# A linear-attention and adapter kernel on one core: the r*k product written over the growth factors of the tile in front, and a new order of the steps

## The chip, the cores and the metric

The kernel runs on one core of a Trainium2 chip. Its metric is the device time of one launch in microseconds (us), the median of several runs. A core has a matrix engine (TensorE, PE in the profile), a vector engine (VectorE, DVE), an activation engine (ScalarE, ACT), a general engine (GpSimd, POOL) and a queue engine (SyncE, SP), each with its own instruction queue that is worked off in order. SBUF is the on-chip memory, PSUM the memory that TensorE writes.

## The reference

The first half is a linear attention with a state that decays per channel (batch 4, 8 heads, 768 steps, head size 48). Its output, plus a mixture of low-rank adapters over 3072 rows of 384, is the result:

```python
for t in range(S):
    kt, vt, rt, wt = k[:, :, t], v[:, :, t], r[:, :, t], w[:, :, t]
    cur = np.einsum('bhd,bhe->bhde', u[None] * kt, vt)
    y[:, :, t] = np.einsum('bhd,bhde->bhe', rt, state + cur)
    state = wt[:, :, :, None] * state + np.einsum('bhd,bhe->bhde', kt, vt)
...
logits = x @ w_gate                      # x: y as rows of 384; 8 experts
topk = np.argpartition(-logits, 2, axis=1)[:, :2]
w = softmax(logits[topk])
delta = sum over the two experts of w[k] * ((x @ A[e]) @ B[e])
return x + delta
```

(The last lines are shortened to what they compute.)

## The kernel before

The 4 x 768 steps are cut into 24 tiles of 128 steps, six for each batch element; a tile holds all 8 heads, 384 columns. Each tile goes through a row of small steps, functions named in the text ORDER: an item `mult.6` is the step `mult` of tile 6. The program is issued in exactly that order, so each engine's queue is the sequence of the items that go to it. The table ENGINES says, by one letter for each tile, which engine does a step that could go to several: D is VectorE, A ScalarE, P GpSimd. The letters of `xkev` start at tile -3.

The steps of tile t, with the line numbers of the profile:

- Loads. `load_w` (SyncE queue), `load_rk` and `load_v` (GpSimd queue, several tiles at a time, converting to 16 bits). Tiles 0 and 1 of r and k come in 32 bits (`load_rkf`, `rk_first`).
- `ln` (ScalarE) takes the logarithm of w for two tiles; `cs` and `ci` (TensorE) sum it up in PSUM; `grow` (L308) and `exps` (L319) on ScalarE turn the two sums into the two halves of a tile `e2` of growth factors, one for r and one for k, in 16 bits.
- `mult` (L336, VectorE) is the decay product: r and k by the two halves of `e2`, in one instruction; `multr` and `mult` of tile 0 do it in two halves (L322). `tr` (L389) transposes the result on TensorE, `trev` copies it out of PSUM (`rkT`; L272 on ScalarE, L274 on VectorE), `amm` (L407) multiplies r with k for each head, and `aev` (L413, VectorE) masks that to `at`.
- `rkp` (L344) is the product r*k of the tile, without growth factors, on VectorE or GpSimd. `xk` of tile t-3 (L466, TensorE) transposes it together with `xs` of tile t-3, `xkev` copies both out, `dgmm` (L349) multiplies with u, `dgev` (two tiles at a time) copies the result `dg` out, and `dv` (L361, GpSimd) multiplies v by it. That is the term of u k v.
- `kv` (L424) adds k v to the state in PSUM, `sev` copies it out; `ymm` (L445, L451) makes the output of the tile, and `xev` (L457, VectorE) adds `dv` to it, which gives `xs`.
- The adapters: `lgmm` the logits, then for four tiles at once (three and one at the end) `gate` (ScalarE, Exp), `gmax` and `gsel` (VectorE, the two best experts), `gmul` (GpSimd, the weights), `zmm` (TensorE), `zw` (VectorE), `zT` and `zTev` (transposed), then for each tile `dmm` (TensorE), `oev` (the result, L592 on VectorE or L590 on ScalarE) and `store` (SyncE queue).

The tile `rkp` has three buffers of its own and `e2` two. A step that writes a buffer waits, by a semaphore, for the readers of what was there.

Of the kernel before, what the change touches and what calls it, by code (L numbers as in the profile page):

```python
# [58 lines left out]
grow.15 xk.11 oev.5 rkp.16 trev.13 dgev.13 xkev.11 dv.12 dmm.7 ci.15 exps.15 dv.13 aev.12 rkp.17 store.2 amm.13
kv.13 oev.6 tr.14 cs.16 sev.13 lgmm.11 oev.7 load_w.20 ymm.12 trev.14 kv.14 aev.13 load_w.22 amm.14 grow.16 zmm.11  # L60
store.3 ci.16 gate.11 xev.12 ln.20 store.4 sev.14 gmax.11 mult.15 exps.16 gsel.11 aev.14 xk.12 tr.15 gmul.11 ymm.13
cs.17 zw.11 mult.16 xkev.12 dgmm.14 trev.15 grow.17 rkp.18 dgmm.15 kv.15 dgev.15 amm.15 ci.17 sev.15 zT.11 tr.16
# [6 lines left out]
xk.17 aev.19 xkev.17 dv.18 tr.20 ymm.18 trev.20 xev.18 rkp.22 zT.15 ci.22 dv.19 lgmm.17 dgmm.20 amm.20 rkp.23
zTev.15 mult.21 store.5 dmm.12 exps.22 aev.20 sev.20 dmm.13 xk.18 oev.12 xkev.18 tr.21 oev.13 ymm.19 trev.21 xev.19  # L70
lgmm.18 cs.23 grow.23 dgmm.21 store.6 amm.21 xk.19 ci.23 ymm.20 dgev.21 dmm.14 xkev.19 mult.22 dv.20 exps.23 aev.21
oev.14 dmm.15 xev.20 dv.21 lgmm.19 gate.19 mult.23 tr.22 trev.22 ymm.21 xk.20 amm.22 kv.21 oev.15 gmax.19 xev.21
xkev.20 sev.21 gsel.19 tr.23 zmm.19 gmul.19 aev.22 trev.23 zw.19 dgmm.22 dgmm.23 dgev.23 amm.23 kv.22 xk.21 zT.19
# [64 lines left out]
def kernel(  # L138
# [167 lines left out]
    def grow(t):  # L306
        e2 = wk.tile([L, 2, HD], BF16, name="e2", bufs=E2_BUFS)
        nc.scalar.activation(out=e2[:, 0], in_=cs_ps[:, 0:HD], func=ACT.Exp)  # L308
        st[t]["e2"] = e2
# [30 lines left out]
        st[t]["rk2"] = rk2  # L340

    def rkp(t):
        p_ = wk.tile([L, HD], FP16, name="rkp", bufs=3)
        (nc.gpsimd if ENGINES["rkp"][t] == "P" else nc.vector).tensor_mul(p_, st[t]["rk"][:, 0], st[t]["rk"][:, 1])  # L344
# [313 lines left out]
```

## Time and profile before

| | |
|---|---|
| median of 3 runs | 94.6 us (93.82 to 94.7) |
| the profiled execution | 93.72 us, with a span of 92.0 us from its first to its last instruction |
| mean granted TensorE clock | 0.991 |
| loads and stores | 17.53 MB in packets, mean 191 GB/s |
| costliest group | `aev`, L413: 24 instructions, 29.2 us on VectorE |
| decay products, L336 on 16-bit tiles | 22 instructions, 14.7 us on VectorE |
| r*k products, L344 on GpSimd | 16 instructions, 15.5 us |
| `dv`, L361 on GpSimd | 24 instructions, 20.4 us |

A line of a timeline in the prediction has the start in us, the duration in us (of all, where several were merged, "x2"), the engine, the line, the operation, the tile written and the tiles read with their shapes, and in brackets how long the engine sat idle before it and what ended that. A line of a group has, after the shapes and the count, the busy time, the mean duration in ns, and the idle time in front. A line with three durations gives the shortest, the middle and the longest in ns. A piece of the chain is a start, a length and what it is. PE is the matrix work, PEld the loading of its weights, which runs beside it. Durations of neighbours on one engine can overlap by some hundredths.

### The profile page before, as it was taken

Reading aid. Unit: us, or ns where it says so; the run is one execution under the profiler, and the core shown is the slowest. Engines: PE = TensorE matmul, PEld = TensorE weight load, DVE = VectorE, ACT = ScalarE, POOL = GpSimd, SP = SyncE. Lnnn points to the kernel's source line nnn. Section 1 sums busy time; section 2 is a strip of 40 time slices with the busy share of each in tenths; the row PEclk is TensorE's granted clock in tenths of the full one; section 3 lists DMA queues with packets and bytes.
Section 4 is the critical chain, followed back from the end, with each engine's and each line's share of the span. In section 5 each row is a group of like instructions: output and inputs, shape, how many; then the busy total and the mean of one; then the engine's idle time right before and its main releaser. Section 6 shows DMA issues by size and latency. Waiting matters only on the chain.

```text
span 92.0 us, 3306 instructions
## 1 busy us (share of the span) xinstructions
PE 79.2 (86%) x1334; PEld 59.8 (65%) x1334; DVE 80.0 (87%) x169; ACT 68.1 (74%) x160; POOL 50.6 (55%) x77
## 2 busy tenths in 40 slices
...
GB/s 27 300 204 278 269 275 261 264 260 275 273 251 218 208 209 215 266 258 260 268 283 268 256 253 247 78 85 110 68 0 85 34 141 89 89 7 185 161 296 46
DMA packets 13599, 17.53 MB, mean 191 GB/s; under 512 B 912, under 2 KB 13328, under 8 KB 13584
## 3 DMA queue, kind: packets, MB, share of 16 engines
...
q10 hardware_dynamic: 144, 0.10, 0.3%
...
## 4 chain that ended last, share of the span: by engine, by line
PE 43%; DVE 40%; issue 6%; ACT 5%; DVEq 0%; POOLq 0%; POOL 0%; ACTq 0%
DVE at L413 13%; DVE xs L457 7%; DVE rk L336 6%; PE trp L389 6%; PE xk_ps L466 5%; PE a_ps L407 5%; PE a_ps L252 4%; DVE res L592 3%; PE y_ps L451 3%; DVE zw L538 3%; PE cs_ps L315 2%; PE y_ps L445 2%; PE cs_ps L304 2%; PE d_ps L572 2%; PE s_ps L424 2%
## 5 line engine op out<-in xcount | busy, mean ns | idle before, releaser
L413 DVE TENSOR_TENSOR at<-a_ps,strict 128x1024 f16<-128x1024 f32 x24 | 29.2, 1215 | 0.9 <-PE a_ps L407 0.9
L361 POOL TENSOR_TENSOR dv<-v,dg 128x384 f32<-128x384 f16 x24 | 20.4, 864 | 13.4 <-ACT dg L266 10.4
L308 ACT ACTIVATE e<-cs_ps 128x384 bf16<-128x384 f32 x24 | 11.8, 493 | 5.9 <-PE cs_ps L304 4.7
L344 POOL TENSOR_TENSOR rkp<-rk 128x384 f16<-128x384 f16 x16 | 15.5, 973 | 1.2 <-POOL rkp L344 0.7
L272 ACT COPY rkT<-trp 128x512 f32<-128x512 f32 (+1 forms) x23 | 13.3, 578 | 3.1 <-PE trp L389 1.9
L336 DVE TENSOR_TENSOR rk<-rk,e 128x768 bf16<-128x768 f16 x22 | 14.7, 675 | 0.8 <-ACT e L319 0.8
L389 PE MATMUL trp<-ident,rk 128*128 128x128 bf16 x184 | 14.1, 219 | 0.9 <-DVE rk L336 0.9
L457 DVE TENSOR_TENSOR xs<-dv,y_ps 128x384 f16<-128x384 f32 x24 | 13.1, 546 | 1.2 <-PE y_ps L451 0.6
L389 PEld LDWEIGHTS <-rk 128*128 128x128 bf16 x184 | 11.1, 97 | 2.4 <-DVE rk L336 1.5
L319 ACT ACTIVATE e<-cs_ps 128x384 bf16<-128x384 f32 x23 | 11.4, 496 | 1.1 <-PE cs_ps L315 0.8
L272 ACT COPY xkT<-xk_ps 128x384 f32<-128x384 f32 (+1 forms) x23 | 10.5, 456 | 2.1 <-PE xk_ps L466 2.0
L407 PE MATMUL a_ps<-rkT 48*128 48x128 bf16 x192 | 9.6, 218 | 1.3 <-DVE at L413 0.9
L266 ACT CAST S_sb<-s_ps 128x384 bf16<-128x384 f32 x18 | 8.8, 487 | 1.0 <-PE s_ps L424 0.8
L281 ACT ACTIVATE logw<-w_in 128x768 f16<-128x768 f32 x11 | 9.3, 846 | 0.0
L451 PE MATMUL y_ps<-v,at 128*128 128x48 f16 x192 | 8.7, 183 | 0.0
L407 PEld LDWEIGHTS <-rkT 48*128 48x128 bf16 x192 | 5.9, 94 | 4.1 <-issue 1.8
L515 POOL TENSOR_TENSOR ge<-ge,den 128x32 f32<-128x32 f32 (+1 forms) x6 | 1.4, 237 | 12.6 <-DVE g L510 10.2
L466 PE MATMUL xk_ps<-ident,xs 128*128 128x128 f16 x72 | 8.0, 220 | 0.3 <-DVE xs L457 0.2
L592 DVE TENSOR_TENSOR res<-d_ps,xs 128x384 f32<-128x384 f32 x15 | 8.0, 549 | 0.2 <-PE d_ps L572 0.2
L304 PE MATMUL cs_ps<-logw,strict 128*128 128x384 f16 x24 | 7.8, 325 | 0.4 <-ACT logw L281 0.4
L466 PE MATMUL xk_ps<-ident,rkp 128*128 128x128 f16 x72 | 7.9, 219 | 0.1
...
## 6 DMA issues: line engine op xcount, KB each, us to landing
...
```

Source lines behind the costliest of these rows:

```text
L272: nc.scalar.copy(out=out.bitcast(F32), in_=in_.bitcast(F32))
L308: nc.scalar.activation(out=e2[:, 0], in_=cs_ps[:, 0:HD], func=ACT.Exp)
L319: nc.scalar.activation(out=st[t]["e2"][:, 1], in_=st[0]["c0"] if t == 0 else cs_ps[:, 0:HD], func=ACT.Exp, scale=-1.0)
L336: nc.vector.tensor_mul(rk2.rearrange("s m p h d -> s (m p h) d")[:, :, 0:D], st[t]["rk"].rearrange("s m (h d) -> s (m h) d", d=D), st[t][" ...
L344: (nc.gpsimd if ENGINES["rkp"][t] == "P" else nc.vector).tensor_mul(p_, st[t]["rk"][:, 0], st[t]["rk"][:, 1])
L361: nc.gpsimd.tensor_mul(dv_, st[t]["v16"], st[t]["dg"].rearrange("p (h o) -> p h o", o=1).to_broadcast([L, H, D]))
L389: nc.tensor.transpose(trp[:, m, p, :], rk2[:, m, p, :, :].rearrange("s a b -> s (a b)"), ident)
L407: nc.tensor.matmul(a_ps[:, g, p, :], lhsT=rkT[base:base + D, 1, p, :], rhs=rkT[base:base + D, 0, p, :], start=True, stop=True)
L413: nc.vector.tensor_mul(at, st[t]["a_ps"].rearrange("s g p f -> s (g p) f"), strict.rearrange("s (o f) -> s o f", o=1).to_broadcast([128, H ...
L451: nc.tensor.matmul(y_ps[:, h, :], lhsT=d["at"][:, g * P + p, :], rhs=d["v16"][:, h, :], start=(c == 0 and h == 0), stop=(h == H - 1), skip ...
L457: nc.vector.tensor_add(xs, st[t]["dv"].rearrange("p a b -> p (a b)"), st[t]["y_ps"].rearrange("p a b -> p (a b)"))
L466: nc.tensor.transpose(xk_ps[:, 3 * q + j, :], src[:, j * 128:(j + 1) * 128], ident16)
```

## The change

`rkp` no longer has buffers of its own. For tile t it writes, as FP16, into the first half (that for r) of the growth factors `e2` of tile t-1, which `mult` of tile t-1 reads; so it waits for that `mult`. Tile 0 writes a constant tile `rkp_first`. `e2` has six buffers in place of two. The text ORDER is replaced by another one, and six rows of ENGINES differ: `rkp` of tile 0 goes to GpSimd and of tile 20 to VectorE; `trev` on VectorE is tile 1 in place of 0 and 7; `xkev` on VectorE is -2, 0, 2 and 3 in place of -3, 2, 3 and 23; `sev` on VectorE is 0 in place of 1 and 3; `dgev` is on VectorE at 9 alone (before at 1 and 9); the results of tiles 2 and 11 go to ScalarE, that of tile 0 to VectorE. Of ORDER the lines are shown that hold steps named here or in the prediction.

```diff
 ORDER = """
-csc.0 warm.0 warm.1 warm.2 warm.3 warm.4 rkp.0 ln.0 warm.5 cs.0 grow.0 ci.0 xk.-3 multr.0 exps.0 trr.0 xkev.-3
-trevr.0 mult.0 load_w1.0 ln1.0 load_w.2 load_rkf.1 tr.0 pad.0 trev.0 load_v.0 load_rk.2 masks.0 load_rk.3 cs.1 amm.0
-grow.1 load_wsb.0 ci.1 exps.1 kv.0 ln.2 sev.0 load_v.2 cs.2 pad.1 grow.2 load_rk.4 load_rk.6 aev.0 load_v.4 rkp.1
...
-load_rk.8 tr.2 rkp.3 ymm.0 grow.3 casts.0 load_v.8 dgev.1 sev.1 aev.1 trev.2 ci.3 kv.2 load_rk.12 load_v.12 amm.2
...
-pad.2 aev.2 load_v.16 trev.3 load_w.8 sev.3 grow.4 ci.4 load_w.10 xkev.0 amm.3 rkp.4 load_w.12 exps.4 dgmm.3 dgev.3
-xk.1 rkp.5 cs.5 xkev.1 dv.2 mult.4 dv.3 ymm.2 grow.5 lgmm.0 tr.4 aev.3 ci.5 xev.2 lgmm.1 ymm.3 rkp.6 ln.6 dgmm.4
-xk.2 exps.5 trev.4 xev.3 cs.6 grow.6 ln.8 xk.3 amm.4 load_v.20 mult.5 tr.5 xkev.2 lgmm.2 dgmm.5 ci.6 trev.5 xkev.3
-exps.6 dgmm.6 lgmm.3 dgev.5 aev.4 gate.3 zmm.3 ln.10 rkp.7 dv.4 cs.7 amm.5 mult.6 tr.6 grow.7 gmax.3 kv.4 ci.7 aev.5
...
-rkp.8 tr.7 sev.6 zT.3 zTev.3 xk.4 load_w.14 aev.6 xkev.4 trev.7 cs.9 ymm.5 grow.9 dmm.0 lgmm.4 xev.5 dmm.1 dgmm.7
...
-xk.5 ci.10 exps.10 dv.6 oev.2 xev.6 kv.8 trev.8 dv.7 rkp.9 mult.9 mult.10 sev.8 xkev.5 ymm.7 cs.11 rkp.10 xk.6 xev.7
-amm.8 kv.9 lgmm.5 dgmm.8 tr.9 grow.11 xkev.6 trev.9 ci.11 dgmm.9 xk.7 lgmm.6 dmm.3 aev.8 load_w.18 exps.11 rkp.11
...
-dgmm.10 ci.13 lgmm.8 dgmm.11 rkp.12 gmul.7 xev.9 xk.9 aev.10 tr.12 exps.13 amm.11 rkp.13 zw.7 dgev.11 zT.7 rkp.14
...
-exps.17 lgmm.12 dv.14 xev.13 ln.22 cs.18 zTev.11 ymm.14 dv.15 grow.18 xk.13 dmm.8 aev.15 trev.16 ci.18 mult.17
...
-cs.19 dgmm.17 trev.17 lgmm.14 dmm.10 grow.19 ymm.15 ci.19 tr.18 oev.9 exps.19 xev.15 kv.18 oev.10 trev.18 amm.17
-mult.19 dgev.17 dv.16 sev.18 cs.20 rkp.20 aev.17 grow.20 dv.17 xk.15 xkev.15 ymm.16 xev.16 ci.20 exps.20 tr.19
...
-oev.16 dmm.17 xev.23 gate.22 gmax.22 oev.17 dmm.18 gsel.22 xk.23 store.7 gmul.22 store.8 oev.18 xkev.23 zmm.22
-zmm.23 lgmm.23 gate.23 store.9 dmm.19 zw.22 zT.22 oev.19 gmax.23 zTev.22 gsel.23 dmm.20 dmm.21 zw.23 oev.20 zT.23
...
+warm.0 warm.1 csc.0 warm.2 warm.3 warm.4 load_w1.0 warm.5 load_v.0 ln.0 load_rk.2 load_rk.3 load_v.2 cs.0 rkp.0 ci.0
...
+sev.0 ln.2 pad.1 cs.2 grow.2 rkp.1 load_rk.8 mult.1 xk.-2 xkev.-2 rkp.2 ci.2 load_v.8 tr.1 exps.2 cs.3 kv.1 cast16.0
...
+trev.3 aev.2 load_v.16 xk.0 grow.4 dgmm.2 pad.2 ci.4 xkev.0 sev.3 rkp.4 amm.3 dgmm.3 load_w.12 exps.4 mult.4 xk.1
+rkp.5 dgev.3 dv.2 dv.3 xkev.1 load_v.20 cs.5 ymm.2 lgmm.0 dgmm.4 aev.3 grow.5 xev.2 lgmm.1 tr.4 ci.5 ln.6 exps.5
+ymm.3 trev.4 cs.6 xk.2 amm.4 mult.5 rkp.6 xev.3 xkev.2 grow.6 ci.6 xk.3 tr.5 dgmm.5 lgmm.2 ln.8 exps.6 trev.5 cs.7
+xkev.3 grow.7 aev.4 lgmm.3 dgmm.6 zmm.3 ci.7 amm.5 gate.3 mult.6 rkp.7 tr.6 gmax.3 ln.10 dgev.5 dv.4 exps.7 aev.5
...
+sev.7 oev.0 dgmm.7 rkp.8 amm.7 load_w.14 exps.9 cs.10 oev.1 dgev.7 tr.8 ymm.6 dv.6 oev.2 grow.10 xk.5 ln.14 dv.7
...
+grow.11 xkev.6 load_w.16 mult.10 ci.11 dmm.3 dgmm.8 rkp.10 xev.7 aev.8 dgmm.9 lgmm.6 xk.7 trev.9 exps.11 dgev.9
+sev.9 amm.9 cs.12 xkev.7 oev.3 rkp.11 tr.10 grow.12 aev.9 load_w.18 ymm.8 mult.11 trev.10 ci.12 lgmm.7 dgmm.10 dv.8
+xev.8 gate.7 exps.12 ymm.9 kv.10 sev.10 dv.9 amm.10 tr.11 gmax.7 xk.8 ln.16 xkev.8 rkp.12 mult.12 cs.13 rkp.13
+grow.13 gsel.7 xev.9 zmm.7 gmul.7 dgmm.11 lgmm.8 store.1 ci.13 xk.9 trev.11 exps.13 tr.12 xkev.9 aev.10 cs.14
...
+rkp.17 trev.16 xkev.13 oev.8 mult.17 amm.16 exps.18 sev.16 store.5 dmm.9 xk.14 cs.19 mult.18 oev.9 tr.17 rkp.18
...
+trev.18 rkp.19 grow.20 dgev.17 sev.18 xk.15 mult.19 ci.20 xkev.15 rkp.20 oev.10 aev.17 exps.20 dv.16 tr.19 ymm.16
...
+gsel.22 dmm.19 xkev.23 gmul.22 lgmm.23 zw.22 zmm.23 zT.22 oev.19 gate.23 store.12 zTev.22 gmax.23 dmm.20 gsel.23
...
 ENGINES = dict(
-    trev="DAAAAAADAAAAAAAAAAAAAAAA",
-    xkev="DAAAADDAAAAAAAAAAAAAAAAAAAD",
-    out="ADDDDADDDDDDADAADAAADDDA",
-    sev="ADADAAAAAAAAAAAAAAAAAAAA",
-    rkp="DDDDDDDPPDPPPPPPPPPPPPPP",
-    dgev="ADAAAAAAADAAAAAAAAAAAAAA",
+    trev="ADAAAAAAAAAAAAAAAAAAAAAA",
+    xkev="ADADADDAAAAAAAAAAAAAAAAAAAA",
+    out="DDADDADDDDDAADAADAAADDDA",
+    sev="DAAAAAAAAAAAAAAAAAAAAAAA",
+    rkp="PDDDDDDPPDPPPPPPPPPPDPPP",
+    dgev="AAAAAAAAADAAAAAAAAAAAAAA",
     zTev="DDDADDDADDDDDDDADDDADDAA",
 )
-E2_BUFS = 2
+E2_BUFS = 6
 RING = 3
 
 
@@ -179,6 +179,7 @@
     def load_wsb(t):
         nc.sync.dma_start(out=w_sb, in_=weights)
 
+    rkp_first = const.tile([L, HD], FP16, name="rkp_first")
     rk_first = const.tile([L, HW_RK, 2, HD], F32, name="rk_first")
 
     def load_rkf(t):
@@ -340,7 +341,7 @@
         st[t]["rk2"] = rk2
 
     def rkp(t):
-        p_ = wk.tile([L, HD], FP16, name="rkp", bufs=3)
+        p_ = st[t - 1]["e2"][:, 0].bitcast(FP16) if t else rkp_first
         (nc.gpsimd if ENGINES["rkp"][t] == "P" else nc.vector).tensor_mul(p_, st[t]["rk"][:, 0], st[t]["rk"][:, 1])
         st[t]["rkp"] = p_
```

More of the change, by code (lines that the diff above doesn't have):

```diff
@@ L59 @@
[L59 to L62, printed above, removed]
-exps.17 lgmm.12 dv.14 xev.13 ln.22 cs.18 zTev.11 ymm.14 dv.15 grow.18 xk.13 dmm.8 aev.15 trev.16 ci.18 mult.17
@@ L69 @@
[L69 to L73, printed above, removed]
@@ new lines @@
+xk.-3 grow.0 multr.0 exps.0 xkev.-3 trr.0 ln1.0 trevr.0 load_w.2 masks.0 load_rkf.1 load_wsb.0 mult.0 adapters.0
+load_rk.4 load_w.4 tr.0 trev.0 pad.0 cs.1 amm.0 load_w.6 grow.1 ci.1 exps.1 load_rk.6 load_w.8 aev.0 kv.0 load_v.4
+sev.0 ln.2 pad.1 cs.2 grow.2 rkp.1 load_rk.8 mult.1 xk.-2 xkev.-2 rkp.2 ci.2 load_v.8 tr.1 exps.2 cs.3 kv.1 cast16.0
+mult.2 load_rk.12 grow.3 trev.1 dgmm.0 dgmm.1 dgev.1 sev.1 ymm.0 rkp.3 casts.0 amm.1 load_v.12 load_w.10 tr.2 ci.3
+aev.1 trev.2 exps.3 kv.2 dv.0 amm.2 ymm.1 sev.2 xev.0 xk.-1 dv.1 ln.4 load_rk.16 mult.3 tr.3 xkev.-1 xev.1 kv.3 cs.4
@@ new lines @@
+trev.3 aev.2 load_v.16 xk.0 grow.4 dgmm.2 pad.2 ci.4 xkev.0 sev.3 rkp.4 amm.3 dgmm.3 load_w.12 exps.4 mult.4 xk.1
+rkp.5 dgev.3 dv.2 dv.3 xkev.1 load_v.20 cs.5 ymm.2 lgmm.0 dgmm.4 aev.3 grow.5 xev.2 lgmm.1 tr.4 ci.5 ln.6 exps.5
+ymm.3 trev.4 cs.6 xk.2 amm.4 mult.5 rkp.6 xev.3 xkev.2 grow.6 ci.6 xk.3 tr.5 dgmm.5 lgmm.2 ln.8 exps.6 trev.5 cs.7
+xkev.3 grow.7 aev.4 lgmm.3 dgmm.6 zmm.3 ci.7 amm.5 gate.3 mult.6 rkp.7 tr.6 gmax.3 ln.10 dgev.5 dv.4 exps.7 aev.5
+kv.4 cs.8 load_rk.20 gsel.3 mult.7 gmul.3 ymm.4 trev.6 sev.4 grow.8 amm.6 ci.8 xev.4 kv.6 ln.12 dv.5 exps.8 tr.7
@@ new lines @@
+sev.6 xk.4 trev.7 cs.9 zw.3 zT.3 ymm.5 kv.7 xkev.4 aev.6 lgmm.4 zTev.3 dmm.0 dmm.1 grow.9 ci.9 xev.5 dmm.2 mult.8
+sev.7 oev.0 dgmm.7 rkp.8 amm.7 load_w.14 exps.9 cs.10 oev.1 dgev.7 tr.8 ymm.6 dv.6 oev.2 grow.10 xk.5 ln.14 dv.7
+ci.10 exps.10 aev.7 xev.6 store.0 kv.8 ymm.7 rkp.9 trev.8 cs.11 xk.6 mult.9 sev.8 xkev.5 amm.8 kv.9 tr.9 lgmm.5
+grow.11 xkev.6 load_w.16 mult.10 ci.11 dmm.3 dgmm.8 rkp.10 xev.7 aev.8 dgmm.9 lgmm.6 xk.7 trev.9 exps.11 dgev.9
+sev.9 amm.9 cs.12 xkev.7 oev.3 rkp.11 tr.10 grow.12 aev.9 load_w.18 ymm.8 mult.11 trev.10 ci.12 lgmm.7 dgmm.10 dv.8
@@ new lines @@
+xev.8 gate.7 exps.12 ymm.9 kv.10 sev.10 dv.9 amm.10 tr.11 gmax.7 xk.8 ln.16 xkev.8 rkp.12 mult.12 cs.13 rkp.13
+grow.13 gsel.7 xev.9 zmm.7 gmul.7 dgmm.11 lgmm.8 store.1 ci.13 xk.9 trev.11 exps.13 tr.12 xkev.9 aev.10 cs.14
+dgev.11 trev.12 zw.7 grow.14 amm.11 zT.7 ymm.10 kv.12 mult.13 load_w.20 store.2 load_w.22 dgmm.12 ci.14 aev.11 dv.10
+zTev.7 ln.18 dmm.4 ymm.11 exps.14 xev.10 xk.10 xkev.10 lgmm.9 cs.15 dv.11 sev.12 oev.4 xev.11 grow.15 amm.12 dmm.5
+dgmm.13 dgev.13 rkp.14 tr.13 lgmm.10 dmm.6 mult.14 xk.11 aev.12 rkp.15 oev.5 dmm.7 trev.13 ci.15 xkev.11 amm.13
@@ new lines @@
+exps.15 kv.13 oev.6 oev.7 sev.13 tr.14 trev.14 cs.16 ymm.12 dv.12 aev.13 mult.15 grow.16 lgmm.11 store.3 kv.14
+gate.11 amm.14 ln.20 dv.13 xev.12 rkp.16 tr.15 xk.12 ci.16 sev.14 exps.16 ymm.13 zmm.11 cs.17 gmax.11 xkev.12
+gsel.11 dgmm.14 dgmm.15 kv.15 aev.14 gmul.11 trev.15 amm.15 grow.17 dgev.15 ci.17 zw.11 dv.14 mult.16 sev.15 xev.13
+store.4 zT.11 zTev.11 tr.16 exps.17 ln.22 lgmm.12 aev.15 cs.18 grow.18 ymm.14 xk.13 dv.15 xev.14 dmm.8 ci.18 kv.16
+rkp.17 trev.16 xkev.13 oev.8 mult.17 amm.16 exps.18 sev.16 store.5 dmm.9 xk.14 cs.19 mult.18 oev.9 tr.17 rkp.18
@@ new lines @@
+xkev.14 ymm.15 grow.19 dgmm.16 ci.19 trev.17 dmm.10 exps.19 dgmm.17 tr.18 lgmm.13 aev.16 cs.20 kv.18 amm.17 xev.15
+trev.18 rkp.19 grow.20 dgev.17 sev.18 xk.15 mult.19 ci.20 xkev.15 rkp.20 oev.10 aev.17 exps.20 dv.16 tr.19 ymm.16
+lgmm.14 lgmm.15 cs.21 trev.19 xev.16 kv.19 gate.15 mult.20 grow.21 gmax.15 amm.18 xk.16 xkev.16 aev.18 dgmm.18 dv.17
+dmm.11 oev.11 ci.21 exps.21 ymm.17 gsel.15 dgmm.19 sev.19 dgev.19 mult.21 zmm.15 cs.22 amm.19 kv.20 ymm.18 grow.22
+sev.20 rkp.21 store.6 xev.17 gmul.15 ci.22 dv.18 store.7 xk.17 exps.22 xkev.17 zw.15 aev.19 tr.20 zT.15 xev.18 cs.23
@@ new lines @@
+lgmm.16 mult.22 dgmm.20 lgmm.17 trev.20 zTev.15 amm.20 dmm.12 grow.23 ci.23 xk.18 oev.12 aev.20 rkp.22 tr.21 dmm.13
+store.8 store.9 ymm.19 xkev.18 trev.21 dgmm.21 exps.23 dgev.21 oev.13 dmm.14 amm.21 dv.19 tr.22 oev.14 xev.19 xk.19
+xkev.19 mult.23 ymm.20 dmm.15 lgmm.18 lgmm.19 rkp.23 dv.20 aev.21 dgmm.22 trev.22 dv.21 ymm.21 tr.23 amm.22 gate.19
+oev.15 store.10 trev.23 kv.21 xev.20 xk.20 gmax.19 zmm.19 xev.21 xk.21 sev.21 xkev.20 xkev.21 dgmm.23 gsel.19 aev.22
+dgev.23 gmul.19 zw.19 dv.22 amm.23 kv.22 zT.19 ymm.22 store.11 sev.22 kv.23 lgmm.20 dv.23 lgmm.21 zTev.19 dmm.16
```

17 lines of the change are left out of this document (3 added, 14 removed).

## Prediction

> **What bounds the kernel now.** I began with the page (busy shares, chain), then took the busy time by stretch, the chain in order of time, VectorE's and GpSimd's timelines side by side, the groups by shape, and the first and last ten microseconds.
>
> ```profile
> span 92.0 us, 3306 instructions
> PE 79.2 (86%) x1334; PEld 59.8 (65%) x1334; DVE 80.0 (87%) x169; ACT 68.1 (74%) x160; POOL 50.6 (55%) x77
> PE 43%; DVE 40%; issue 6%; ACT 5%; DVEq 0%; POOLq 0%; POOL 0%; ACTq 0%
> ...
> 10.00:20.00 10.00, 9.05 (x148) 6.46 (x147) 9.05 (x17) 8.99 (x21) 5.49 (x8) 1.00 1.14 264
> 20.00:38.00 18.00, 16.18 (x287) 11.87 (x286) 17.76 (x32) 14.96 (x34) 10.62 (x14) 1.00 1.19 239
> 38.00:65.00 27.00, 26.74 (x508) 21.70 (x505) 26.44 (x55) 25.05 (x60) 16.82 (x22) 1.00 0.91 218
> ...
> 39.80 0.40 PE a_ps L407 x8
> ...
> 64.63 0.21 PE cs_ps L315
> ```
>
> The stretch rows give, after the length, busy microseconds of PE, PE loads, DVE, ACT, POOL. From 20 to 38 us VectorE is the limit: busy 17.76 of 18, while TensorE has 1.82 us idle. From 38 to 65 TensorE is busy 26.74 of 27, and between the two chain pieces shown, the first and last of that stretch, the chain never leaves it (VectorE, 26.44, is nearly as full). So a microsecond saved on VectorE can pay before 38 us, hardly from 38 to 65, and again afterwards.
>
> The second thing to see is that some VectorE instructions take far longer than their like, each while GpSimd computes:
>
> ```profile
> L336 DVE TENSOR_TENSOR rk<-rk,e x22: 527/552/1355, 13.3 to 76.2; 128x768 bf16<-128x768 f16 x22
> L344 DVE TENSOR_TENSOR rkp<-rk x6: 348/352/803, 12.1 to 35.7; 128x384 f16<-128x384 f16 x6
> L336 DVE TENSOR_TENSOR rk<-rk,e 128x768 bf16<-128x768 f16 x22 | 14.7, 675 | 0.8 <-ACT e L319 0.8
> ...
> 22.46 1.35 DVE L336 TENSOR_TENSOR rk<-rk,e 128x768 bf16<-128x768 f16 x1
> 22.47 0.93 POOL L344 TENSOR_TENSOR rkp<-rk 128x384 f16<-128x384 f16 x1
> 25.66 0.82 POOL L361 TENSOR_TENSOR dv<-v,dg 128x384 f32<-128x384 f16 x1 [2.27 <-ACT dg L266]
> 25.80 1.10 DVE L336 TENSOR_TENSOR rk<-rk,e 128x768 bf16<-128x768 f16 x1
> 35.37 1.90 POOL L344 TENSOR_TENSOR rkp<-rk 128x384 f16<-128x384 f16 x2
> 35.69 0.80 DVE L344 TENSOR_TENSOR rkp<-rk 128x384 f16<-128x384 f16 x1
> 36.42 1.73 DVE L336 TENSOR_TENSOR rk<-rk,e 128x768 bf16<-128x768 f16 x2
> 41.38 0.56 DVE L336 TENSOR_TENSOR rk<-rk,e 128x768 bf16<-128x768 f16 x1
> 41.48 1.23 POOL L344 TENSOR_TENSOR rkp<-rk 128x384 f16<-128x384 f16 x1
> 65.36 0.82 POOL L361 TENSOR_TENSOR dv<-v,dg 128x384 f32<-128x384 f16 x1
> 65.38 1.22 DVE L336 TENSOR_TENSOR rk<-rk,e 128x768 bf16<-128x768 f16 x1
> ```
>
> The middle of the three figures in the first two rows is the usual time (the third row has the decay products' mean, 675 ns): 0.55 us for a decay product (mult), 0.35 for an r*k product (rkp) on VectorE. Against a GpSimd rkp the excess is 1.35-0.55 = 0.80, 0.80-0.35 = 0.45 and 1.73-1.10 = 0.63, together 1.88 us, all between 22 and 38. Against a GpSimd dv it is 0.55 and 0.67, together 1.22. Where VectorE came first by 0.10 us (41.38), it kept its 0.56 and GpSimd stretched from 0.93 to 1.23.
>
> **The new order of rkp.** In the changed kernel rkp of tile t writes where mult of tile t-1 reads, so it cannot start before that mult ends. The three collisions above break this rule: 22.47 is rkp.7 beside mult.5, and 35.37 is rkp.10 and rkp.11 beside rkp.9, mult.9 and mult.10. All three must go: 1.88 us. What can stand in their place is rkp.t beside mult.t. In VectorE's new queue mult.t comes later than the 0.93 us of a product behind mult.t-1, save where two mults stand back to back: 9 with 10, 17 with 18 (13 and 14 of the old queue are parted). There GpSimd is released when the next mult is already next in line; I take the row 41.38 (VectorE keeps its time, 0) over 22.46 (0.80). The Trainium skill, "SBUF — State Buffer", section "SBUF: two separate sides", calls the port pair that VectorE and GpSimd share an exclusive lock, held for a whole instruction by whichever starts first. By it the waiting mult wins and the sum stays; the row 41.38 agrees, the row 22.46, where VectorE's record starts first and still loses, does not show it.
>
> The wait has things behind it: in GpSimd's queue gmul.7 stands behind rkp.13, dv.16 and dv.17 behind rkp.18 and rkp.19, dv.8 behind rkp.11; TensorE's xk.(t-3) waits for rkp.t. Between mult.(t-1) and the xev.(t-3) that the same xk needs, VectorE has at least a mult and an xev, mostly an at product besides, so the product is covered; only xk.7 is short, by some 0.3 us, and four other matmul steps stand ahead of it. Cost 0; without that cover 0.3 once. Six buffers of growth factors in place of two only take waits away, and the trace names none for them: 0.
>
> **Work moved between engines.**
>
> ```profile
> L268 DVE CAST S_sb<-s_ps 128x384 bf16<-128x384 f32 x2 | 1.1, 553 | 0.0
> L274 DVE COPY xkT<-xk_ps 128x768 f16<-128x768 f16 x2 | 1.0, 544 | 0.0
> L274 DVE COPY xkT<-xk_ps 128x384 f16<-128x384 f16 x2 | 0.7, 351 | 0.0
> L274 DVE COPY rkT<-trp 128x1024 bf16<-128x1024 bf16 x1 | 0.7, 681 | 0.0
> L592 DVE TENSOR_TENSOR res<-d_ps,xs 128x384 f32<-128x384 f32 x15 | 8.0, 549 | 0.2 <-PE d_ps L572 0.2
> ```
>
> Start, to 10 us. VectorE loses rkp.0, xkev.-3 and trev.0.
>
> ```profile
> 4.56 0.56 DVE L344 TENSOR_TENSOR rkp<-rk_first 128x384 f16<-128x384 f32 x1 [0.67 <-DMA rk_first<-in_rk_dram]
> 6.16 0.33 PE L466 MATMUL xk_ps<-ident,rkp 128*128 128x128 f16 x3
> 7.33 0.40 PE L367 MATMUL trp<-ident,rk 128*128 128x128 bf16 x4 [0.85 <-DVE rk L322]
> ...
> 7.27 0.27 DVE xkT L274
> ```
>
> The last row is a piece of the chain: mult.0 stood behind that copy, which is now on ScalarE: -0.27. rkp.0 goes to GpSimd, behind four load issues. From 4.56 even two of its 0.93 us products end at 6.4, and the transposes behind it on TensorE (7.33) are not due for 0.9 more: 0.
>
> From 10 to 22 us VectorE gains sev.0 0.55, xkev.-2 0.35, trev.1 0.68, xkev.0 0.54 and loses sev.1 and sev.3 at 0.55 each and a 16-column copy: about +0.9, against 0.95 us idle there (10-9.05). Between 0 and +0.9 I take +0.4, also for the rkp instructions that now wait for the mult right in front.
>
> From 22 to 38 us VectorE loses trev.7, 0.68; oev.0 and oev.2 change places. With the 1.88 that is 2.56 us off the engine that sets this stretch. TensorE caps it:
>
> ```profile
> 23.88 0.62 PE L389 MATMUL trp<-ident,rk 128*128 128x128 bf16 x8 [0.43 <-DVE rk L336]
> 26.96 0.62 PE L389 MATMUL trp<-ident,rk 128*128 128x128 bf16 x8 [0.50 <-DVE rk L336]
> 37.73 0.31 PE L424 MATMUL s_ps<-v,rk 128*64 128x48 f16 x8 [0.51 <-DVE rk L336]
> ```
>
> Its waits for stretched mults are 1.44 us, its whole idle time there 1.82. I take the middle, -1.63; what is late next is TensorE itself. The loads set a floor too:
>
> ```profile
> L191 POOL DMA_DIRECT2D rk<-in_rk_dram x1: 785/785/785, 7.2 to 7.2; - x1
> ...
> DMA to landing us min/median/max: 23.2/23.2/23.2
> ...
> 32.70 0.55 DVE L336 TENSOR_TENSOR rk<-rk,e 128x768 bf16<-128x768 f16 x1
> ```
>
> The rk tiles 8 to 11, issued at 7.2, land at 30.4; mult.8 used them at 32.70, so it may move up 2.3 us. The sum asks for 0.80+0.55+0.68 = 2.03 at most by then: no cost.
>
> From 38 to 65 us: 0, TensorE's work is the same. After that oev.11 leaves VectorE (-0.55) and rkp.20 comes (+0.35): -0.20.
>
> The end:
>
> ```profile
> 83.16 0.86 ACT L590 COPY res<-d_ps 128x384 f32<-128x384 f32 x2 [0.17 <-PE d_ps L572]
> 83.76 0.35 DVE L274 COPY xkT<-xk_ps 128x384 f16<-128x384 f16 x1
> 84.66 0.18 ACT L486 ACTIVATE ge<-s_ps 128x8 f32<-128x8 f32 x1 [0.64 <-POOL g L516]
> ```
>
> xkev.23 moves to ScalarE, behind the two result copies (to 84.02), so it ends some 0.25 later than 84.11; gate.23, the 84.66 row, is now queued behind oev.19. Between 0 and +0.5, I take +0.25.
>
> Sum: -0.27 +0.40 -1.63 -0.20 +0.25 = -1.45 us. The dv collisions (1.22) I leave as many as they were. The profiled execution took 93.72 us for its span of 92.0; from it the sum gives 92.3. The median of the three runs shown is 94.6, 0.9 above; the same sum from there gives 93.15, and I forecast 93.1 as a median.
>
> **Rivals.** *The back-to-back mults lose the port.* If rkp.10 and rkp.18 win as rkp.7 did at 22.47, mult.10 costs 0.80 again, and mult.18, inside TensorE's full stretch, 0 to 0.80. For it is that very pair of rows, against it 41.38. It gives 93.9 to 94.7, say 94.3: no change.
>
> *The collisions move to dv.* A dv is released by a ScalarE copy, not by a mult, and nothing in the change orders it. The new queues bring five pairs close: rkp.5 behind mult.4 with dv.2, mult.7 with dv.4, mult.13 with dv.10 or dv.11, mult.19 with dv.16, rkp.20 with dv.17. Each costs about 0.61 (mean of 0.55 and 0.67). From the fifth extra one on the gain is gone and over 1% lost: 93.1+5x0.61 = 96.15, less some of VectorE's 0.56 us idle between 38 and 65: 95.9, slower. For it: two of the four collision sites are dv's already. Against it: all five would have to fall within 0.8 us.
>
> *All of it goes.* With the late dv collision gone too (0.67) and TensorE's idle time filled (0.19 more) the time is 92.2.
>
> *The order was there anyway.* If GpSimd's own queue already held rkp behind mult, only the moves remain: 94.6-0.27+0.40-0.68-0.20+0.25 = 94.1. The rows 22.47 and 35.37 speak against it.
>
> **How the numbers follow.** Forecast 93.1: 0.47. All goes, 92.2: 0.08. Port lost, 94.3: 0.17. Order there anyway, 94.1: 0.03. Moved to dv, 95.9: 0.25. About 1% is what a measurement of this kernel tells from no change, so faster means below 93.65: 0.55; same: 0.20; slower, above 95.55: 0.25. The range reaches down to 91.8 (92.2 with the +0.4 of the early stretch at nothing) and up to 96.0 to take in the dv case. The likeliest case alone spans 92.4 to 93.6.
>
> **What would show it.** The mults' longest time falls from 1355 ns towards 0.6 us outside dv collisions, their mean from 675 to under 610; GpSimd's rkp records start behind the mult in front; TensorE's waits for mult between 20 and 38 shrink from 1.44 us to under 0.5; mult.10 ends near 36.4 instead of 38.15; the stretch of 27 us behind it keeps its length. The forecast is wrong if mults stretch beside dv as often as five times more, if TensorE waits at xk for rkp, if a load holds rkp or mult before 31 us, or if the last 10 us grow by over 0.5.

## The result, and the profile after

| | before | changed |
|---|---|---|
| median of 20 runs each, us | 94.12 (93.5 to 94.8) | 93.5 (93.13 to 93.95) |
| ratio to before, 95% interval | | 0.9933 (0.9906 to 0.996) |
| profiled execution, us | 93.72 | 93.14 |
| its span, us | 92.0 | 91.4 |

The change gains 0.6 us, 0.7%. The interval tells that from no gain, but it is within the 1% that the prediction counts as no change; the forecast was 93.1, a gain of 1.45. The ratios here and below leave out runs that took over 1.5% longer than the fastest of the same kernel; the medians are of all runs. Most of the gain that was foreseen is there at 37 us. It is then lost in one place that the prediction did not look at.

The page and the busy time by stretch of the changed kernel (length, PE, PE loads, DVE, ACT, POOL); line numbers are one higher than before:

```profile
span 91.4 us, 3313 instructions
PE 79.3 (87%) x1335; PEld 59.1 (65%) x1335; DVE 76.9 (84%) x165; ACT 69.0 (75%) x164; POOL 50.3 (55%) x77
PE 47%; DMA 19%; DVE 14%; ACT 8%; issue 4%; SPq 2%; ACTq 0%; DVEq 0%
```

```profile
10.00:20.00 10.00, 8.70 (x145) 5.91 (x143) 8.99 (x17) 8.21 (x19) 5.39 (x8) 1.00 1.14 264
20.00:38.00 18.00, 16.83 (x304) 12.95 (x302) 17.15 (x34) 16.21 (x37) 10.32 (x14) 1.00 1.19 236
38.00:65.00 27.00, 25.81 (x493) 20.71 (x491) 25.31 (x53) 24.30 (x59) 16.52 (x23) 1.00 0.88 211
```

VectorE is busy 3.1 us less, and its share of the chain falls from 40% to 14%; loads, which the chain of before did not contain, now hold 19%. They are two, here as pieces of the chain (start, length): one of r and k at the start, and one of w.

```profile
2.65 8.49 DMA rk_first<-in_rk_dram
...
34.02 9.15 DMA w_in<-in_w_dram
```

From 38 to 65 us TensorE, busy 26.74 us before, is busy only 25.81: that stretch now has a hole.

VectorE's groups in the changed kernel (shortest, middle, longest in ns) and GpSimd's rkp (busy, mean | idle in front):

```profile
L337 DVE TENSOR_TENSOR rk<-rk,e x22: 542/551/623, 13.1 to 74.1; 128x768 bf16<-128x768 f16 x22
L345 DVE TENSOR_TENSOR e<-rk x7: 348/351/869, 12.8 to 63.5; 128x384 f16<-128x384 f16 x7
...
L345 POOL TENSOR_TENSOR e<-rk 128x384 f16<-128x384 f16 x15 | 14.0, 935 | 12.2 <-DVE rk L337 9.6
```

No mult is stretched any more (longest 623 ns, was 1355), and GpSimd now idles in front of rkp until a mult has ended, 9.6 us in all. One rkp on VectorE, 869 ns, still collides. The hole has these lines (SyncE's queue, ScalarE, TensorE, VectorE in the timeline; the brackets tell what ended the idle time; the last line is the time from issue to landing of the load issued at 34.02):

```profile
33.62 0.36 SPq L600 DMA_DIRECT2D out_dram<-res  x1
34.02 0.53 SPq L174 DMA_DIRECT2D w_in<-in_w_dram  x1
...
43.19 0.84 ACT L282 ACTIVATE logw<-w_in 128x768 f16<-128x768 f32 x1 [1.48 <-DMA w_in<-in_w_dram]
44.46 0.23 PE L350 MATMUL s_ps<-w,xkT 128*128 128x8 f16 x3 [1.11 <-ACT xkT L273]
45.73 0.56 DVE L337 TENSOR_TENSOR rk<-rk,e 128x768 bf16<-128x768 f16 x1 [1.12 <-ACT e L320]
```

```profile
DMA to landing us min/median/max: 9.1/9.1/9.1
```

Read the first block upwards from the bottom: mult.13 waits for its growth factors, TensorE for a copy, and both for ScalarE, which stands for 1.48 us at ln.16 until the load of w for tiles 16 and 17 has landed, 34.02 + 9.1 = 43.1. SyncE's queue is worked off in order: that load stands behind store.0, and store.0 waits for oev.0.

The table gives the start of the at product (aev) of some tiles, in us, in each profiled execution; each entry is one row of VectorE's timeline. The difference between two columns tells where time went. One profiled execution stands for each kernel, so tenths of a microsecond at aev.0 mean little (see the start, below).

| kernel | aev.0 | aev.4 | aev.8 | aev.10 | aev.11 | aev.17 | aev.23 | span |
|---|---|---|---|---|---|---|---|---|
| before | 9.65 | 24.67 | 38.53 | 44.05 | 46.05 | 63.75 | 80.02 | 92.0 |
| changed | 9.14 | 25.18 | 37.24 | 42.80 | 46.65 | 64.25 | 79.24 | 91.4 |
| w_early | 9.50 | 26.38 | 38.43 | 43.99 | 46.34 | 63.93 | 78.92 | 91.1 |
| w_early_rkp5 | 8.90 | 24.01 | 36.91 | 42.78 | 45.12 | 62.72 | 77.71 | 89.9 |
| own_buf_w_early | 9.32 | 25.69 | 38.48 | 44.42 | 47.05 | 66.15 | 81.08 | 93.5 |
| old_wait_w_early | 10.62 | 24.84 | 37.91 | 43.50 | 45.43 | 64.64 | 81.75 | 93.7 |

From aev.10 to aev.11 the kernel before takes 2.00 us, the changed one 3.85: the 1.25 us by which it was ahead are gone, and 0.6 more.

### The profile page after: what moved, and what is told of

Its sections match the earlier page's. It is cut to its first block, busy times and chain, and to the rows that moved or that the text cites. A ratio compares the mean times of both kernels' runs of the same rounds, so it can differ in the third digit from the quotient of the medians.

```text
span 91.4 us, 3313 instructions
## 1 busy us (share of the span) xinstructions
PE 79.3 (87%) x1335; PEld 59.1 (65%) x1335; DVE 76.9 (84%) x165; ACT 69.0 (75%) x164; POOL 50.3 (55%) x77
## 3 DMA queue, kind: packets, MB, share of 16 engines
q1 hardware_dynamic: 7312, 10.55, 35.5%
## 4 chain that ended last, share of the span: by engine, by line
PE 47%; DMA 19%; DVE 14%; ACT 8%; issue 4%; SPq 2%; ACTq 0%; DVEq 0%
DMA w_in<-in_w_dram 10%; DMA rk_first<-in_rk_dram 9%; PE trp L390 8%; PE xk_ps L467 6%; PE a_ps L408 5%; DVE at L414 5%; PE d_ps L573 3%; PE y_ps L452 3%; PE z_ps L524 3%; DVE rk L337 3%; PE cs_ps L316 3%; PE s_ps L425 3%; DVE xs L458 2%; PE cs_ps L304 2%; PE cs_ps L305 2%
## 5 line engine op out<-in xcount | busy, mean ns | idle before, releaser
L362 POOL TENSOR_TENSOR dv<-v,dg 128x384 f32<-128x384 f16 x24 | 20.2, 859 | 10.4 <-ACT dg L267 10.2
L345 POOL TENSOR_TENSOR e<-rk 128x384 f16<-128x384 f16 x15 | 14.0, 935 | 12.2 <-DVE rk L337 9.6
L337 DVE TENSOR_TENSOR rk<-rk,e 128x768 bf16<-128x768 f16 x22 | 12.0, 554 | 1.4 <-ACT e L320 1.4
L267 ACT CAST S_sb<-s_ps 128x384 bf16<-128x384 f32 x19 | 9.3, 487 | 0.6 <-PE s_ps L425 0.4
L467 PE MATMUL xk_ps<-ident,e 128*128 128x128 f16 x69 | 7.6, 219 | 0.5 <-DVE e L345 0.5
L316 PE MATMUL cs_ps<-logw,ident 128*128 128x384 f16 x23 | 7.5, 326 | 0.3 <-ACT e L309 0.2
L452 PEld LDWEIGHTS <-at 128*128 128x128 f16 x192 | 7.0, 96 | 1.0 <-DVE at L414 0.8
L593 DVE TENSOR_TENSOR res<-d_ps,xs 128x384 f32<-128x384 f32 x14 | 7.4, 552 | 0.1
```

Of the source, the lines that this page charges most:

```text
L337: nc.vector.tensor_mul(rk2.rearrange("s m p h d -> s (m p h) d")[:, :, 0:D], st[t]["rk"].rearrange("s m (h d) -> s (m h) d", d=D), st[t][" ...
L362: nc.gpsimd.tensor_mul(dv_, st[t]["v16"], st[t]["dg"].rearrange("p (h o) -> p h o", o=1).to_broadcast([L, H, D]))
L452: nc.tensor.matmul(y_ps[:, h, :], lhsT=d["at"][:, g * P + p, :], rhs=d["v16"][:, h, :], start=(c == 0 and h == 0), stop=(h == H - 1), skip ...
L467: nc.tensor.transpose(xk_ps[:, 3 * q + j, :], src[:, j * 128:(j + 1) * 128], ident16)
```

## The experiments

Times are medians. The kernels ran on three chips, each with runs of the kernel before on the same chip: w_early, old_w_early, own_buf and own_buf_w_early (kernel before: 94.2 us); w_early_rkp5, w5_tail, old_wait and old_wait_w_early (94.41); out_back, rkp5_alone and w16_rkp5 (94.01). So the ratio is what compares across chips.

### The load of w out of the store's shadow

```diff
+load_w.16 load_w.18
 store.0
...
-load_w.16
...
-load_w.18
```

**w_early**, the changed kernel with this edit.

> The changed kernel, with the loads of w for tiles 16 to 19 put ahead of the first store in SyncE's queue. Theory (the gain is made by 40 us and lost at ln.16, which waits 1.48 us for a load that stood behind store.0): no wait at ln.16, the at product of tile 11 at about 45.2 us in place of 46.65, and 92.0 us, 1.5 less than the changed kernel. Rival (the new order itself is late there, mult.13 being queued ahead of the at product of tile 11): VectorE still idles about a microsecond at mult.13 and the time stays at 93.4. Rival (the DMA engines are full, so the early loads hold up others): a wait for rk or v appears before 40 us and the time is 93.5 or more.

Measured: 92.5 us, ratio 0.9804 (0.9745 to 0.9863), against 0.9933 for the change alone. In its trace ln.16 no longer waits, and TensorE is full again:

```profile
42.80 0.85 ACT L282 ACTIVATE logw<-w_in 128x768 f16<-128x768 f32 x1
```

```profile
38.00:65.00 27.00, 27.00 (x522) 21.87 (x518) 26.72 (x55) 25.76 (x62) 18.25 (x24) 1.00 0.91 204
```

aev.10 to aev.11 takes 2.35 us, and VectorE does not idle at mult.13: the rival that blamed the new order there falls. 0.5 us less came than expected, and aev.11 starts at 46.34, not 45.2, because this execution comes to aev.8 only at 38.43, 1.19 us behind the changed one. Two things in the trace bear on that: rkp.5 had a longer collision (the group on rkp.5, below), and the early loads pushed others. v of tiles 8 to 11, issued at 10.2, landed 25.3 us later, at 35.5, where it took 22.3 in the changed kernel. With the lead gone before the load was due, this pair of kernels alone would not tell what the load is worth; rkp5_alone and w16_rkp5, below, differ in that load alone.

**old_w_early**, the same edit on the kernel before.

> The kernel before with the loads of w for tiles 16 to 19 ahead of the first store. Its ln.16 did not wait (load landed at 41.75, used at 42.55). Theory (that load limits only the changed kernel): 94.1, no change within 0.3 us. Rival (the loads behind the store slow both kernels alike): 0.5 us or more faster.

Measured: 94.21 us, ratio 0.9994 (0.9953 to 1.0036). The load limits only the changed kernel.

**out_back**: the loads stay; the results of tiles 0 and 2 go back to the engines that they had.

```diff
-    out="DDADDADDDDDAADAADAAADDDA",
+    out="ADDDDADDDDDAADAADAAADDDA",
```

> The changed kernel with the results of tiles 0 and 2 on the engines of the kernel before (tile 0 on ScalarE, tile 2 on VectorE). Theory (moving the result of tile 0 to VectorE, behind mult.8, is what sent its store, and the load of w behind it, out at 33.6 and 34.0 in place of 32.9 and 33.35): the load is issued about 0.6 us earlier, the wait at ln.16 falls from 1.5 to about 0.9, and the time to about 93.0. Rival (the longer landing, 9.1 us for 8.4, and an earlier ScalarE make the wait): wait and time as they are, 93.5.

Measured: 93.03 us, ratio 0.9904 (0.9847 to 0.9962).

```profile
33.29 0.36 SPq L600 DMA_DIRECT2D out_dram<-res  x1
33.70 1.36 SPq L174 DMA_DIRECT2D w_in<-in_w_dram  x2
...
43.08 0.84 ACT L282 ACTIVATE logw<-w_in 128x768 f16<-128x768 f32 x1 [1.04 <-DMA w_in<-in_w_dram]
```

The load is issued 0.32 us earlier, where 0.6 was expected, and takes 9.4 us to land (the changed kernel: 9.1), so it lands at 43.1 as there. The wait still falls from 1.48 to 1.04, because ScalarE comes 0.33 us later (42.04 against 41.71): this execution was 0.38 us behind by aev.3 (21.49 against 21.11). Counted from aev.3 the load is issued 0.70 us earlier and ln.16 starts 0.5 earlier. The ratio overlaps that of the changed kernel (0.9906 to 0.996). Theory and rival each have a part, and how much of the wait the move of oev.0 makes stays open.

### The wait of rkp for mult

**own_buf** and **own_buf_w_early**: rkp in buffers of its own again, with the order of the changed kernel; the second with the loads early.

```diff
-        p_ = st[t - 1]["e2"][:, 0].bitcast(FP16) if t else rkp_first
+        p_ = wk.tile([L, HD], FP16, name="rkp", bufs=6)
```

> The changed kernel with rkp in six buffers of its own again, so that it waits for no mult; order and engines as in the changed kernel. Theory (the wait is what parts rkp from mult): mults and rkp's of 0.8 us and more come back at 22 to 37 us, the mults' mean goes from 554 ns to over 600, and the at product of tile 8 starts 0.8 to 1.9 us later than 37.24; because ln.16 waits for its load until 43.2 in any case, the end moves by only 0 to 0.6 us: 93.5 to 94.1. Rival (the new queues part them without the wait): mults as before at 554 ns, 93.5 us.

> Both edits: rkp in its own buffers and the loads of w early. Theory: with the load's floor gone the collisions show in full, 0.8 to 1.9 us over the kernel with the early loads alone, 92.8 to 93.9. Rival (the wait is worth nothing): the same time as with the early loads alone.

Measured: 95.47 us, ratio 1.0137 (1.0081 to 1.0192), and 95.47 us, ratio 1.0127 (1.008 to 1.0174). Without the wait the new order is slower than the kernel before; with the loads early the wait is worth 95.47-92.5 = 3.0 us. From the second one's trace:

```profile
L337 DVE TENSOR_TENSOR rk<-rk,e 128x768 bf16<-128x768 f16 x22 | 15.4, 707 | 0.3 <-ACT e L320 0.3
```

```profile
22.54 0.92 POOL L345 TENSOR_TENSOR rkp<-rk 128x384 f16<-128x384 f16 x1
22.55 1.34 DVE L337 TENSOR_TENSOR rk<-rk,e 128x768 bf16<-128x768 f16 x1
...
59.81 2.10 POOL L345 TENSOR_TENSOR rkp<-rk 128x384 f16<-128x384 f16 x2
...
60.28 2.04 DVE L337 TENSOR_TENSOR rk<-rk,e 128x768 bf16<-128x768 f16 x2
```

The mults' mean is 707 ns, (707-553) x 22 = 3.4 us over the kernel with the wait (its mean is 553): about the 3.0 us. In own_buf aev.8 starts at 38.81, 1.57 us later than in the changed kernel, as the theory had it, but the end moved much further: its size was too small, because it looked for collisions before 37 us alone. With the loads early, 2.17 us arise from aev.8 to aev.17 (27.67 against 25.50 in w_early), where the prediction let VectorE's time count for little. The pair at 60.28, mult.17 and mult.18 beside rkp.18 and rkp.19, is new and falls into TensorE's stretch, which it lengthens: from aev.15 to aev.16 it takes 4.50 us there (58.22 to 62.72), 3.46 in w_early (57.55 to 61.01).

**old_wait** and **old_wait_w_early**: the opposite half, the wait without the new order.

```diff
-        p_ = wk.tile([L, HD], FP16, name="rkp", bufs=3)
+        p_ = st[t - 1]["e2"][:, 0].bitcast(FP16) if ENGINES["rkp"][t] == "P" else wk.tile([L, HD], FP16, name="rkp", bufs=3)
...
-E2_BUFS = 2
+E2_BUFS = 6
...
-rkp.7
...
 mult.6
+rkp.7
```

(and the same for rkp.14 to rkp.19, rkp.22 and rkp.23 behind the mult of the tile in front)

> The kernel before, with its own order and engines; GpSimd's rkp's alone write over the growth factors of the tile in front, six buffers of those, and the nine rkp's that stood ahead of that tile's mult in the order stand right behind it. Theory (the wait itself makes the gain, the new order little of it): the stretched products at 22.46, 35.69 and 36.42 go, those beside dv at 25.80 and 65.38 may stay; 1.4 to 1.9 us less on VectorE by 38 us, of which the load of w used at 42.55 and landed at 41.75 lets 0.8 through: about 93.3. Rival (in the old order the later rkp's hold dv and gmul back): 94.2 or more.

> That, with the loads of w for tiles 16 to 19 ahead of the first store. Theory: without the load's floor the whole of it comes through, 92.3 to 92.8, as good as the changed kernel with early loads (92.5). Rival (the new order makes the gain): 93.5 or more.

Measured: old_wait 95.17 us, of twelve runs that lie in two groups, six from 93.6 to 94.79 and six from 95.54 to 96.45; ratio 0.9971 (0.9927 to 1.0016), no gain that can be told from none. old_wait_w_early 95.49 us, ratio 1.0146 (1.0101 to 1.0191): there the rival holds clearly. The table shows both halves of why: counted from aev.0, the wait brings aev.8 from 28.88 to 27.29 (28.87 in old_w_early, which has the early loads without the wait), the 1.6 us that the theory gave it; the lead is lost from aev.14 on. There the lines of old_wait_w_early read:

```profile
54.64 0.92 POOL L343 TENSOR_TENSOR e<-rk 128x384 f16<-128x384 f16 x1 [2.39 <-DVE g L509]
55.51 0.24 POOL L514 TENSOR_TENSOR ge<-ge,den 128x32 f32<-128x32 f32 x1
55.83 0.25 POOL L515 TENSOR_TENSOR g<-g,ge 128x32 f32<-128x32 f32 x1
56.12 0.69 DVE L537 TENSOR_TENSOR zw<-z_ps,g 128x512 f16<-128x512 f32 x1 [0.73 <-POOL g L515]
...
58.30 1.61 POOL L360 TENSOR_TENSOR dv<-v,dg 128x384 f32<-128x384 f16 x2
59.12 1.20 DVE L335 TENSOR_TENSOR rk<-rk,e 128x768 bf16<-128x768 f16 x1
```

rkp.16, put behind mult.15, now stands right ahead of gmul.11 in GpSimd's queue and holds it back, so VectorE waits 0.73 us at zw.11; dv.14 and dv.15 come late behind rkp.17 and meet mult.17. Why the spread of old_wait is so wide, and why the early loads slowed it, was not settled.

### The rkp that still collides

**w_early_rkp5**: rkp.5, on VectorE, moved from behind mult.4 to behind xev.2, on top of w_early.

```diff
 mult.4
...
-rkp.5
...
 xev.2
+rkp.5
```

The lines that it was meant to remove, first in the changed kernel, then in w_early:

```profile
19.95 1.92 POOL L362 TENSOR_TENSOR dv<-v,dg 128x384 f32<-128x384 f16 x2 [0.88 <-ACT dg L267]
20.32 0.87 DVE L345 TENSOR_TENSOR e<-rk 128x384 f16<-128x384 f16 x1
```

```profile
20.44 1.94 DVE L345 TENSOR_TENSOR e<-rk 128x384 f16<-128x384 f16 x1
20.52 1.62 POOL L362 TENSOR_TENSOR dv<-v,dg 128x384 f32<-128x384 f16 x2
```

> The changed kernel with the loads of w early, and rkp.5 on VectorE put behind xev.2 instead of right behind mult.4, so that it no longer meets dv.2 and dv.3. Theory (a VectorE product that meets dv waits for it, and in this kernel that reaches the end): rkp.5 takes 0.35 us in place of 0.87 to 1.94, the at product of tile 3 starts near 20.4, and the end comes 0.5 to 1.6 us earlier than with the early loads alone (92.5): 90.9 to 92.0. Rival (TensorE or a later load takes it back): 92.5.

Measured: 91.81 us, ratio 0.9734 (0.9688 to 0.978). That is below w_early's 0.9804, but the two intervals overlap. The at product of tile 3 follows mult.4 at once:

```profile
19.14 0.56 DVE L337 TENSOR_TENSOR rk<-rk,e 128x768 bf16<-128x768 f16 x1 [0.27 <-ACT e L320]
19.61 1.22 DVE L414 TENSOR_TENSOR at<-a_ps,strict 128x1024 f16<-128x1024 f32 x1
```

**rkp5_alone**: the same move on the changed kernel, its loads as they were.

> The changed kernel with rkp.5 behind xev.2, the loads of w where the change has them. Theory (whatever is gained by 40 us is taken by the wait for the load of w, which itself hangs on the result of tile 0 and the store behind it): VectorE is up to a microsecond ahead at the at product of tile 3 and the store of tile 0 goes out that much earlier, so the load lands earlier by the same and 0.3 to 0.9 us come through: 92.6 to 93.2. Rival (the floor is a fixed bandwidth, not the queue): 93.5.

Measured: 92.63 us, ratio 0.9877 (0.9822 to 0.9931).

```profile
32.88 0.36 SPq L600 DMA_DIRECT2D out_dram<-res  x1
33.28 1.01 SPq L174 DMA_DIRECT2D w_in<-in_w_dram  x2
...
42.80 0.84 ACT L282 ACTIVATE logw<-w_in 128x768 f16<-128x768 f32 x1 [1.83 <-DMA w_in<-in_w_dram]
```

The collision's end brings oev.0, its store and the load forward: the load is issued 0.74 us earlier than in the changed kernel. It lands, after 9.5 us, only 0.3 to 0.4 earlier, so the rival has a part too, and ln.16 starts at 42.80 in place of 43.19. ScalarE waits longer than there, 1.83 us, and yet the ratio is lower, 0.9877 against 0.9933, with intervals that overlap. As far as these tell, a floor that hangs on the kernel's own progress hides part of a gain, not all of it. The move of rkp.5 lowers the ratio by 0.006 to 0.007 in both pairs, each time about as much as the intervals leave open; with the early loads it is clear of the changed kernel.

**w16_rkp5**: one load of w ahead of the first store instead of two.

> The changed kernel with rkp.5 behind xev.2 and one load of w, that of tiles 16 and 17, ahead of the first store; the next stays behind it. With both ahead the v of tiles 8 to 11 landed at 35.05, and TensorE waited 1.1 us for it. Theory (the loads share one full bandwidth, so half the bytes ahead push v half as far): v lands near 33.7, TensorE waits at most 0.2 us, and the time is 91.0 to 91.5, 0.3 to 0.8 less than with both loads early. Rival (that wait was covered, or the next load of w becomes late): 91.8 or more.

Measured: 91.84 us, ratio 0.978 (0.9734 to 0.9825): not faster than with both. Against rkp5_alone, on the same chip, the one difference is where the load of w for tiles 16 and 17 stands, and its worth is the difference of the medians, 92.63-91.84 = 0.8 us: the slowest run here, 92.11 us, is ahead of the fastest there, 92.15. From aev.8 to aev.17 it takes 25.47 us here (37.31 to 62.78) and 27.35 there (36.49 to 63.84). v landed at 10.5+24.0 = 34.5, and TensorE no longer waited for it, but the time stayed: that wait was covered. Here and in w_early_rkp5 TensorE is busy 27.00 of the 27 us from 38 to 65, so what reached it a little sooner only queued there.

**w5_tail**: w_early_rkp5 with the last tile's steps as in the kernel before.

```diff
-    xkev="ADADADDAAAAAAAAAAAAAAAAAAAA",
+    xkev="ADADADDAAAAAAAAAAAAAAAAAAAD",
...
-lgmm.22 dmm.17 dmm.18 zmm.22 xk.23 dmm.19 xkev.23 lgmm.23 zmm.23 oev.19 gate.23 dmm.22 zT.23
+lgmm.22 dmm.17 dmm.18 xk.23 zmm.22 xkev.23 zmm.23 lgmm.23 dmm.19 gate.23 oev.19 zT.23 dmm.22
```

(the items concerned, in their sequence)

> The same, and the last tile's steps as in the kernel before: xkev.23 on VectorE, xk.23 ahead of zmm.22, gate.23 ahead of oev.19, zT.23 ahead of dmm.22. Theory (the new tail gave back 0.40 us between the at product of tile 23 and the last result: 0.78 ahead there, 0.38 ahead at the end): 0.25 to 0.45 us faster than the kernel without it. Rival (the end is set by the last products on VectorE and the last store): no change.

Measured: 91.76 us, ratio 0.9731 (0.9686 to 0.9776): no difference from the 0.9734 without it; the rival holds. This kernel, w_early_rkp5 and w16_rkp5 are as fast as one another within their intervals and faster than both kernels of the study, by 2.2 to 2.7% over the one before.

## Why the prediction was right in its mechanism and too high in its size

- **The rkp collisions go, and with them 1.88 us.** Right. They are gone from the trace; own_buf_w_early shows them returning without the wait, and old_wait_w_early shows the wait removing 1.6 us by aev.8 without the new order. TensorE's waits for stretched mults from 20 to 38 us, 1.44 us before, are gone with them.
- **Back-to-back mults keep the port.** Right in both places. The pairs mult.9, mult.10 and mult.17, mult.18 take 1.02 us each, their usual length, and GpSimd's first product behind them is the one that stretches:

```profile
35.84 1.02 DVE L337 TENSOR_TENSOR rk<-rk,e 128x768 bf16<-128x768 f16 x2
36.53 1.97 POOL L345 TENSOR_TENSOR e<-rk 128x384 f16<-128x384 f16 x2 [1.32 <-DVE rk L337]
```

- **10 to 22 us, +0.40, and 22 to 38 us, -1.63.** The two together, -1.23, came as -0.78 from aev.0 to aev.8 (28.88 us before, 28.10 changed). The table's cut at aev.4 (+1.02 and -1.80) lies behind the collision at 22.46, which the prediction counted in the second term, so the terms are compared with a cut ahead of it, at xev.2. These are mult.4, aev.3 and xev.2, first before, then changed:

```profile
19.66 0.55 DVE L336 TENSOR_TENSOR rk<-rk,e 128x768 bf16<-128x768 f16 x1
20.13 1.22 DVE L413 TENSOR_TENSOR at<-a_ps,strict 128x1024 f16<-128x1024 f32 x1
21.27 0.54 DVE L457 TENSOR_TENSOR xs<-dv,y_ps 128x384 f16<-128x384 f32 x1
```

```profile
19.72 0.56 DVE L337 TENSOR_TENSOR rk<-rk,e 128x768 bf16<-128x768 f16 x1 [0.27 <-ACT e L320]
...
21.11 1.21 DVE L414 TENSOR_TENSOR at<-a_ps,strict 128x1024 f16<-128x1024 f32 x1
22.24 0.54 DVE L458 TENSOR_TENSOR xs<-dv,y_ps 128x384 f16<-128x384 f32 x1
```

The first term, from aev.0 to xev.2, is 11.62 against 13.10 us, +1.48: much too small in the forecast. In time the changed kernel is 0.06 us behind at mult.4 and 0.98 at aev.3; in between stands rkp.5, which the new order put behind mult.4, and 0.52 of it is rkp.5 stretched beside dv.2, the first of the five pairs of the dv rival and the only one that came. The forecast itself has none of the five; they are priced in the rival alone. The second term, from xev.2 to aev.8, is 17.26 against 15.00, -2.26: larger than forecast by 0.63, and 0.55 of that is the collision with dv at 25.80, which went although the prediction left it as it was.
- **Start, -0.27.** Not to be told apart. aev.0 starts at 9.14, but in w_early, w_early_rkp5, rkp5_alone and w16_rkp5, whose steps up to there are the same, at 9.50, 8.90, 8.76 and 9.32. And in this execution the lead at aev.0 (0.51 us) went at once: rkp.1 stood waiting for a load until 11.23 (it starts at 10.79 in the kernel before), one of the signs that the prediction had named for being wrong.

```profile
11.23 0.56 DVE L345 TENSOR_TENSOR e<-rk_first 128x384 f16<-128x384 f32 x1 [0.40 <-DMA rk_first<-in_rk_dram]
```

- **38 to 65 us, 0.** This is the step that failed. From aev.8 to aev.17 the kernel before takes 25.22 us, the changed one 27.01, +1.79. "TensorE's work is the same" was true, and did not answer whether its input comes in time. The prediction looked at one load only, the rk of tiles 8 to 11, and priced "oev.0 and oev.2 change places" at nothing, by VectorE's balance alone. oev.0 carries store.0, and store.0 carries the next loads of w in SyncE's queue. In the timeline of before, and in the time from issue to landing of the load issued at 33.35, the margin could be read:

```profile
33.35 0.60 SPq L174 DMA_DIRECT2D w_in<-in_w_dram  x1
...
42.55 0.87 ACT L281 ACTIVATE logw<-w_in 128x768 f16<-128x768 f32 x1
```

```profile
DMA to landing us min/median/max: 8.4/8.4/8.4
```

Landed at 41.75, used at 42.55: a margin of 0.8 us. In the changed kernel ScalarE is ready for ln.16 at 43.19-1.48 = 41.71, which uses up the margin and no more. The wait comes from the load, which lands 1.4 us later, at 43.1: it is issued 0.67 us later and takes 0.7 longer to land. How much of this the move of oev.0 makes, and why the landing takes longer, the runs do not settle (out_back). That the load's place makes the loss is shown: with it moved the stretch takes 25.50 us (w_early) and 25.47 (w16_rkp5).
- **After that, -0.20.** Larger: from aev.17 to aev.23 16.27 against 14.99, 1.28 less. The late collision with dv (0.67 us at 65.38) went too, which the forecast had left as it was; where the remaining 0.4 comes from was not tried.
- **The end, +0.25.** +0.18 by the spans, 11.98 against 12.16 us behind aev.23; w5_tail shows that undoing it brings nothing measurable.

The terms measured add up: -0.51+1.48-2.26+1.79-1.28+0.18 = -0.60, the difference of the spans. That the forecast of 93.1 lies only 0.4 us from the median is partly luck. Its start was 94.6, the median of three runs; from the 94.12 of twenty runs the same sum gives 92.67, 0.8 off. And its misses partly cancel: +1.08 for 10 to 22 us and +1.79 for 38 to 65, -0.63 for 22 to 38 and -1.08 after 65. Of the rivals the chance given to "slower" hung on five collisions with dv and one came; no rival had the load of w.
